# Decay attention and two expert layers on one core: another instruction order, decay rows written by engines

## The chip, the cores and the metric

One Trainium2 chip, one of its cores. A core has TensorE (PE: matmuls and transposes, with a weight load PEld ahead of each), VectorE (DVE), ScalarE (ACT), GpSimd (POOL) and SyncE (SP), on whose queue this kernel puts its DMAs. The metric is the device time of one execution in microseconds (us), as the median of several.

## The reference

```python
scores = scale * np.matmul(q, k.transpose(0, 1, 3, 2))      # 4 x 8 heads, 576 x 64
cum = np.cumsum(np.log(np.clip(f, 0.0001, 1.0)), axis=-1)
decay = cum[:, :, :, None] - cum[:, :, None, :]
scores = np.where(causal, -1000000000.0, scores + decay)
scores = scores - np.max(scores, axis=-1, keepdims=True)
attn = np.exp(scores)
attn = attn / (np.sum(attn, axis=-1, keepdims=True) + 1e-09)
x = np.matmul(attn, v)                                      # as 2304 tokens x 512
h = x @ w_in1                                               # 512 x 2048, expert layer 1
g = np.where(h >= 1, h, np.where(h <= -1, 0.0, (h + 1) ** 2 / 4))
x = g @ w_out1                                              # 2048 x 512
h = x @ w_in2                                               # expert layer 2
P = a[0] + a[1] * h + a[2] * h * h + a[3] * h * h * h
Q = 1.0 + np.abs(b[0]) * np.abs(h) + np.abs(b[1]) * h * h
out = (P / (Q + 1e-06)) @ w_out2
```

## The kernel before

Every operand of a large matmul is split into a high part, rounded to the type fp32r, and the low rest; a product is then three matmuls: low by high, high by low, high by high.

**Attention** goes through 16 pairs of heads (two heads side by side on the 128 partitions). For each pair ScalarE rounds k and q (`hi`: kh, qh), VectorE or GpSimd takes the rests (`lo`: kl, ql), and qdh/qdl hold the last 64 queries of both heads. The 576 queries are nine blocks of scores, the last one first. For a block TensorE issues the score matmuls (tiles S); VectorE adds mask and decay from `cb` and takes the row's extreme in one instruction (`max_fn`, tiles P and nm); ScalarE takes the exponential and the row sum (tile ls); TensorE transposes the block in parts of 128 (`t_fn`, tiles T, two PSUM buffers), and ScalarE or VectorE copies each transposed part to SBUF (`c_fn`, tiles PT). Then follow the products with v (tasks V, tiles O). The row sums are inverted in `r1` (a 128x9 addition of 1e-9, then the reciprocal), turned by TensorE (R2), sent through HBM and spread over the partitions (R), and GpSimd multiplies the pair's output xa by them (`r6`).

The decay of pairs 1 to 15 comes to `cb` from HBM (`cd`, which ScalarE's `c_all` fills and one DMA stores; `load_c` reads it). Pair 0 does without that trip: its decay enters the scores as a fourth matmul, of a matrix of ones with the decay rows `ct`. The cumulative sums `cum` lie in the tile `ft` (32 rows, one for each head); `c_hi` writes -8 cum rounded to fp32r, `c_lo` the rest, and two DMAs (`load_c(0)`) bring them to `ct`, whose other rows are zero. `one` is all ones, `oned` holds ones in rows 0, 1 (columns 0 to 63) and 64, 65 (columns 64 to 127). GpSimd makes these tiles with memsets.

While waiting for the first data TensorE runs `warm` matmuls on a tile of zeros, WARM + WARM2 = 26 of them.

**The expert layers** follow: layer 1 in passes over chunks of tokens (tiles h, g, a), layer 2 with its first product by a scheme of seven products of quarters, its second as three matmuls (tiles b), all behind attention except that the first matmuls of layer 1 are mixed into attention's later pairs. On the way the weights are unpacked (`w_steps`), split and stored. `root_steps` are ten small instructions (128x1) on |b[1]|, which layer 2 needs late: a square root by logarithm and exponential and two corrections.

**The order.** Every piece of work is a `task(key, engine, duration, function, deps, take, free)`. `plan` draws up a timetable from the durations given: again and again it takes, of all ready tasks, the one with the least start time plus `wk` times its key, and then the program is emitted in the order of the planned starts. So a duration in the list decides only the order; each engine runs its instructions in that order, as soon as what they depend on is done. The engine name "dve" is VectorE; "dvp" is VectorE too, but such a task and GpSimd's tasks exclude each other in the plan:

```python
at = max(clock[OF.get(eng, eng)], free_at, port[0] if eng in SHARED else 0.0)   # SHARED = ("dvp", "pool")
...
turn = SWC if ways[0][0] == "pe" and shape.get(n) != at_shape[0] else 0.0
cand = (choice[1] + turn + wk * key, key, n, choice[1], choice[2])
...
if eng == "pe" and shape.get(n) != at_shape[0]:
    at_shape[0] = shape.get(n)
    dur += SWT
```

SWC and SWT are the planned price of a turn between matmuls that take all of TensorE's rows and columns and those that take half of the rows or half of the columns. The table `NUDGE` adds an amount to the keys of runs of tasks, by their numbers.

Of the kernel before, what the change touches and what calls it, by code (L numbers as in the profile page):

```python
# [18 lines left out]
def kernel(ctx, tc, qT, kT, v, f, w_in1, w_out1, w_in2, w_out2, a, b, out):  # L19
# [9 lines left out]
    P = 128  # L29
# [21 lines left out]
    WARM, WARM2 = 12, 14  # L51
    WK = 0.025
    SWC, SWT = 0.1, 0.19
# [156 lines left out]
    POOL.memset(oned[:].bitcast(F32), 0.0)  # L210
    for j in range(2):
        pp = slice(j * QB, (j + 1) * QB)
        POOL.memset(half[pp, j:j + 1], 1.0)
        POOL.memset(oned[j * QB:j * QB + 2, pp].bitcast(F32), 1.0)
    POOL.memset(one[:].bitcast(F32), 1.0)
    POOL.memset(ct[0][:].bitcast(F32), 0.0)
# [20 lines left out]
    def load_c(pr):  # L237
        if not pr:
            for x in range(2):
                SP.dma_start(ct[0][x:P:QB, :].bitcast(F32), ft[0:2, 2 + x, :].bitcast(F32))  # L240
            return
# [26 lines left out]
    def task(key, eng, dur, fn, deps=(), take=(), free=()):  # L268
# [31 lines left out]
    ]  # L300

    def nudge(first):
        for n0, count, by_ in NUDGE:
            for n in range(max(n0, first), min(n0 + count, len(tasks))):
                if first or tasks[n][0] > -50:
                    tasks[n] = (tasks[n][0] + by_, *tasks[n][1:])
# [100 lines left out]
    def tasks_of_pair(pr):  # L407
# [37 lines left out]
        if pr:  # L445
            T("ldc", kl + 1, "sp", DC, lambda: load_c(pr), ((0, "stored"),), ("cb",))
        else:
            T("ldc", -99, "sp", [(0.55, 0.05)] * 2, lambda: load_c(pr), ((0, "c"),), ("cb",))
# [9 lines left out]
        for pos, (b, j) in enumerate(BLOCKS):  # L458
# [8 lines left out]
            def s_fn(s=s, b=b, both=both, cuts=cuts):  # L467
                if both:
                    St[s] = []
                    for n0, n1 in cuts:  # L470
                        t = psS.tile([P, 512], F32, tag="S", name=f"S{s}_{n0}")
                        ways = [(qdl[:], kh[:, n0:n1]), (qdh[:], kl_[:, n0:n1]), (qdh[:], kh[:, n0:n1])]
                        if pr == 0:
                            ways.append((oned[0:QB + 2], c_[0:QB + 2, n0:n1]))
# [98 lines left out]
        for g in (1, 0):  # L573
# [5 lines left out]
            for c in range(ncs):  # L579
# [15 lines left out]
                T(f"V{g}{c}", s0 + last + KV, "pe", mm(n - c_q, 4) + 0.03, pv_fn,  # L595
# [44 lines left out]
        T("R1", kr, "dvp", 0.25, r1, [f"E{p}" for p in range(NB)])  # L640
        T("R2", kr + 1, "pe", 0.2, r2, ("R1",), ("T",))
# [14 lines left out]
    NH = B * H  # L656
    ft = ap1.tile([NH, 4, S], F32R, tag="PT1", name="ft")
    zt = ap1.tile([NH, S], F32, tag="PT0", name="zt")
    SP.dma_start(ft[:, 0, :].bitcast(F32), f.rearrange("b h s -> (b h) s"))
# [20 lines left out]
    cum = ft[:, 1, :].bitcast(F32)  # L680

    def c_hi():
        ACT.activation(ft[:, 2, :], cum, AF.Copy, scale=-ROOT)

    def c_all():
        ACT.activation(ft[:, 0, :].bitcast(F32), cum, AF.Copy, scale=-ROOT)

    def c_lo():
        DVE.scalar_tensor_tensor(
            out=ft[:, 3, :], in0=cum, scalar=-ROOT, in1=ft[:, 2, :].bitcast(F32), op0=ALU.mult, op1=ALU.subtract  # L690
# [30 lines left out]
    x = ft[:, 0, :].bitcast(F32)  # L721
# [4 lines left out]
    t = task(-99, "act", 0.57, c_hi, (t,))  # L726
    t2 = task(-98, "act", 0.57, c_all, (t,))
# [788 lines left out]
```

## Time and profile before

| | |
|---|---|
| time, 3 runs | median 957.78 us (956.24 to 957.89) |
| the profiled execution | 958.39 us, of which the profile's span is 956.7 us |
| TensorE's mean granted clock | 0.995 |
| busy share: TensorE, VectorE, ScalarE, GpSimd | 98%, 79%, 74%, 48% |
| bytes moved by DMA | 188.55 MB, 197 GB/s |

The profile records one execution. Busy shares are of the span. The granted clock is told in parts of full speed: 1.0 is 2.4 GHz, 0.5 is 1.2 GHz. L551 in a row is line 551 of the kernel that ran. A row such as `T<-P` names the tile written and the tiles read; `[1.23 <-DVE nm]` is idle time ahead of the instruction and what ended it.

### The profile page before, as it was taken

To read this page: it belongs to the slowest core of one execution; us is meant where nothing else is said; L and a number is where in the kernel's file an instruction comes from. 1 tells how busy PE (TensorE), PEld (TensorE's weight loads), DVE (VectorE), ACT (ScalarE), POOL (GpSimd) and SP (SyncE) were. 2 spreads that over 40 slices of the span, in tenths; PEclk is the share of its full clock that TensorE was granted. 3 is DMA by queue.
4 is the path that set the end of the run, shared out by engine and by line. 5 is a ranking of instruction groups with operands and counts; after the bars stand their busy time and mean duration, and the time that the engine had idled before them with its cause. 6 is when DMAs were issued, how large, how long until landed. Compare 5 with 4: busy or idle time off the path is not lost.

```text
span 956.7 us, 16614 instructions
## 1 busy us (share of the span) xinstructions
PE 938.7 (98%) x5172; PEld 791.6 (83%) x5172; DVE 758.6 (79%) x1614; ACT 706.1 (74%) x1568; POOL 462.3 (48%) x542
## 2 busy tenths in 40 slices
PE   9899999999999999999999999999999999999998
PEld 6576877778888888878998878989899988989986
DVE  8989889983766987897658598899988888888840
ACT  7789888985665655655556589889897889878752
POOL 3666733645565422222222166666555567455553
PEclk9989999999999999999999999999999999999999
DMA  8778799755554478577947846767434464334100
GB/s 261 229 231 270 245 293 291 247 179 209 177 175 144 140 262 284 187 250 260 329 142 251 283 161 200 253 231 258 143 133 143 142 216 144 118 137 165 34 34 34
DMA packets 107345, 188.55 MB, mean 197 GB/s; under 512 B 13092, under 2 KB 43188, under 8 KB 107256
## 3 DMA queue, kind: packets, MB, share of 16 engines
q1 hardware_dynamic: 107256, 187.48, 59.0%
q8 instruction: 41, 0.67, 0.3%
q14 instruction: 48, 0.39, 0.1%
HBM read 142.72 MB, written 44.71 MB: 196 GB/s over the span
## 4 chain that ended last, share of the span: by engine, by line
PE 81%; DVE 9%; DMA 5%; ACT 2%; issue 2%; SPq 0%; DVEq 0%; ACTq 0%
PE b L1055 20%; PE h L1029 17%; PE h L777 17%; PE a L879 15%; PE T L551 3%; PE O L588 3%; PE S L485 2%; PE a L868 2%; DMA cb<-cd 1%; DVE P L527 1%; DMA wqd<-t 1%; DVE wd L109 1%; DVE arena L1000 1%; PE S L476 1%; DMA qs<-in_q_dram 1%
## 5 line engine op out<-in xcount | busy, mean ns | idle before, releaser
L798 POOL TENSOR_TENSOR gl<-t,gh 128x512 fp32r<-128x512 f32 (+2 forms) x125 | 146.7, 1179 | 213.5 <-ACT gh L793 176.3
L1055 PE MATMUL b<-w,gh 128*128 128x512 f32 x576 | 179.1, 392 | 0.0
L879 PE MATMUL a<-gh,w 128*128 128x512 f32 (+1 forms) x576 | 161.8, 366 | 0.0
L832 POOL TENSOR_TENSOR t<-t,t 128x384 f32<-128x384 f32 x96 | 99.3, 1037 | 94.9 <-ACT t L825 93.4
L1055 PEld LDWEIGHTS b<-w,gh 128*128 128x128 f32 x576 | 108.0, 188 | 21.1
L777 PE MATMUL h<-xh,arena 128*128 128x512 f32 (+1 forms) x400 | 120.0, 368 | 0.5 <-DVE t L814 0.5
L879 PEld LDWEIGHTS a<-gh,w 128*128 128x128 f32 x576 | 104.0, 189 | 17.1
L1055 PE MATMUL b<-w,gl 128*128 128x512 f32 x288 | 112.1, 389 | 0.5 <-DVE osb L399 0.5
L793 ACT CAST gh<-t 128x512 fp32r<-128x512 f32 (+2 forms) x125 | 68.8, 553 | 50.9 <-PE a L879 17.9
L879 PE MATMUL a<-gl,w 128*128 128x512 f32 (+1 forms) x288 | 105.4, 366 | 0.6 <-DVE t L890 0.5
L1029 PE MATMUL h<-arena,q 128*128 128x384 f32 x459 | 93.5, 337 | 2.9 <-DVE h L1043 1.5
L539 ACT ACTIVATE P<-P,nm 128x576 f32<-128x576 f32 (+2 forms) x144 | 83.8, 583 | 16.0 <-DVE nm L527 15.5
L814 DVE SCALAR_TENSOR_TENSOR t<-h,t 128x512 f32<-128x512 f32 (+1 forms) x77 | 47.2, 630 | 55.1 <-ACT t L809 54.9
L1029 PEld LDWEIGHTS h<-arena,q 128*128 128x128 f32 x459 | 81.1, 188 | 8.4 <-issue 1.9
L777 PEld LDWEIGHTS h<-xh,arena 128*128 128x128 f32 x400 | 73.1, 189 | 13.4 <-DVE t L814 0.9
L804 ACT ACTIVATE t<-h 128x512 f32<-128x512 f32 (+1 forms) x77 | 42.4, 551 | 50.1 <-PE h L777 49.0
L250 POOL TENSOR_SCALAR_AFFINE_SELECT cb<-cb 128x128 f32<-128x128 f32 (+1 forms) x150 | 51.0, 353 | 58.2 <-DVE nm L527 56.0
L777 PE MATMUL h<-xl,arena 128*128 128x512 f32 (+1 forms) x200 | 73.6, 368 | 0.0
L551 PE MATMUL T<-ident,P 128*128 128x128 f32 x400 | 64.7, 285 | 6.0 <-DVE PT L399 3.8
L527 DVE CUSTOM_DVE_ANT_0 P<-S,cb 128x256 f32<-128x256 f32 (+1 forms) x135 | 62.3, 476 | 7.4 <-issue 2.0
L822 ACT ACTIVATE t<-h,ab 128x384 f32<-128x384 f32 x96 | 56.1, 584 | 13.6 <-DVE h L1043 12.8
L551 PEld LDWEIGHTS T<-ident,P 128*128 128x128 f32 x400 | 46.1, 143 | 20.4 <-DVE PT L399 5.0
(185 smaller groups left out, 2332.7 us busy)
## 6 DMA issues: line engine op xcount, KB each, us to landing
q<-wqd SPq DMA_DIRECT2D x46, 512.0 KB, 3.7
raw<-in_moe_w_in_dram SPq DMA_DIRECT2D x32, 512.0 KB, 5.6
raw<-in_moe_w_out_dram SPq DMA_DIRECT2D x32, 512.0 KB, 3.8
arena<-wqd SPq DMA_DIRECT2D x26, 512.0 KB, 3.7
cb<-cd SPq DMA_DIRECT2D x15, 576.0 KB
xr<-xd SPq DMA_DIRECT2D x32, 256.0 KB, 3.6
wqd<-t SPq DMA_DIRECT2D x32, 256.0 KB, 3.8
wfd<-wd SPq DMA_DIRECT2D x26, 256.0 KB
```

Of the source, the lines that this page charges most:

```text
L250: POOL.affine_select(out=t, in_=t, compare_op=ALU.is_ge, fill=-BIG, base=0, pattern=[[-1, n]], channel_multiplier=1,)
L527: DVE.tensor_tensor_reduce(out=p[:, n0:n1], in0=t[:, 0:n1 - n0], in1=m, scale=-1.0 / ROOT, scalar=least, op0=ALU.add, op1=ALU.min, accum_o ...
L539: ACT.activation(p, p, AF.Exp, scale=-1.0, bias=nm[pr][:, pos:pos + 1], accum_out=ls[pr][:, COL[pos]:COL[pos] + 1])
L551: PE.transpose(ps[:, (c - c0) * P:(c - c0 + 1) * P], p[:, k0:k0 + P], ident[:])
L777: PE.matmul(hps[g], ww[:, kk * P:(kk + 1) * P], xx[kk], start=(kk == 0 and y == 0), stop=(kk == KD - 1 and y == 2))
L793: ACT.copy(gt[g][0], mid[g][0][:, 0:n])
L798: eng.tensor_tensor(out=lo, in0=t[:, 0:lo.shape[1]], in1=hi.bitcast(F32), op=ALU.subtract)
L822: ACT.activation(mid[g]["w"], hps[g], AF.Abs, scale=ab[:, 0:1])
L832: POOL.tensor_tensor(out=vv, in0=vv, in1=mid[g]["w"], op=ALU.add)
L879: PE.matmul(acc[x, d], ww[:, dd], gg, start=(first and y == 0), stop=(last and y == 2))
L1029: PE.matmul(o, ww, xx, start=(new and i == 0 and z == 0), stop=(i == HQ - 1 and z == 2), skip_group_check=True,)
L1055: PE.matmul(acc[x, d], gg[:, dd], ww, start=(g == 0 and y == 0), stop=(g == NF - 1 and y == 2))
```

## The change

1. Warm-up: WARM2 from 14 to 9, so 21 warm-up matmuls in place of 26.
2. First decay rows: `c_hi` and `c_lo` now write into `ct` (rows 0 to 31 high, 32 to 63 low, 64 to 95 high again, 96 to 127 a copy of the low rows by ScalarE). The two DMAs are gone. `one` is now 1 in four rows only, 0 and 32 (the first head's high and low row) and 65 and 97 (the second head's): four GpSimd instructions of 32x128 write a column of `ident` over 128 columns. `oned` takes two 64x64 copies of `one`. The fourth score matmul of the first block now uses 128 rows in place of 66. The clearing of `ct` is gone.
3. `c_all` and the store of `cd` go from keys -98 and -97 to -60.
4. In the list of durations: a V task is 4 (n - c_q) / 2400 + 0.015 in place of 4 (n / 2400 + 0.013) + 0.03, R1 is 0.33 (0.25), R2 0.12 (0.2), SWT 0.1 (0.19).
5. The root steps of VectorE are planned as "dvp".
6. The very last output tile's copy out of PSUM is done in two halves, ScalarE and VectorE.
7. `NUDGE` has 86 entries (51 before), and each has a step, so that it may shift every 77th task.

```diff
     CS = 12.0
-    WARM, WARM2 = 12, 14
+    WARM, WARM2 = 12, 9
     WK = 0.025
-    SWC, SWT = 0.1, 0.19
+    SWC, SWT = 0.1, 0.1
...
     POOL.memset(oned[:].bitcast(F32), 0.0)
+    NH = B * H
     for j in range(2):
...
         POOL.memset(half[pp, j:j + 1], 1.0)
-        POOL.memset(oned[j * QB:j * QB + 2, pp].bitcast(F32), 1.0)
-    POOL.memset(one[:].bitcast(F32), 1.0)
-    POOL.memset(ct[0][:].bitcast(F32), 0.0)
+        for x in range(2):
+            r0 = j * QB + x * NH
+            rows = slice(r0, r0 + NH)
+            POOL.tensor_scalar(
+                out=one[rows, :], in0=ident[rows, r0 + j:r0 + j + 1].to_broadcast([NH, P]), scalar1=1.0, scalar2=None,
+                op0=ALU.mult,
+            )
+        POOL.tensor_scalar(out=oned[pp, pp], in0=one[pp, pp].bitcast(F32), scalar1=1.0, scalar2=None, op0=ALU.mult)
...
     def load_c(pr):
-        if not pr:
-            for x in range(2):
-                SP.dma_start(ct[0][x:P:QB, :].bitcast(F32), ft[0:2, 2 + x, :].bitcast(F32))
-            return
         t = cb[pr % 2]
...
         for j in range(2):
...
     NUDGE = [
-        (1307, 58, 1.3), (1243, 58, 6.2), (792, 35, -3.0), (618, 16, -8.4), (1400, 59, 0.8), (884, 3, 5.1),
...
+        (23, 27, 7.2, 1), (1322, 49, 21.1, 1), (1204, 3, 2.4, 77), (57, 8, -20.5, 77), (1430, 18, 5.5, 1),
...
     ]
...
     def nudge(first):
-        for n0, count, by_ in NUDGE:
-            for n in range(max(n0, first), min(n0 + count, len(tasks))):
-                if first or tasks[n][0] > -50:
+        for n0, count, by_, step_ in NUDGE:
+            for n in range(n0, min(n0 + count * step_, len(tasks)), step_):
+                if n >= first and n0 >= first and (first or tasks[n][0] > -50):
                     tasks[n] = (tasks[n][0] + by_, *tasks[n][1:])
...
         else:
-            T("ldc", -99, "sp", [(0.55, 0.05)] * 2, lambda: load_c(pr), ((0, "c"),), ("cb",))
+            T("ldc", -99, "act", 0.57, lambda: ACT.copy(ct[0][P - NH:P, :], ct[0][NH:2 * NH, :].bitcast(F32)), ("c", "c2"), ("cb",))
         ways, lo_, qd_ = (["dvp", "pool"], [0.68, 1.42], [0.24, 0.4]) if pr else (["dvp"], [0.68], [0.24])
...
             kk += 15 * x * (not pr)
...
                         if pr == 0:
-                            ways.append((oned[0:QB + 2], c_[0:QB + 2, n0:n1]))
+                            ways.append((oned[:], c_[:, n0:n1]))
                         for x, (lhs, rhs) in enumerate(ways):
...
                         St[s].append((t, n0, n1))
...
-                T(f"V{g}{c}", s0 + last + KV, "pe", mm(n - c_q, 4) + 0.03, pv_fn,
+                T(f"V{g}{c}", s0 + last + KV, "pe", 4 * (n - c_q) / 2400 + 0.015, pv_fn,
                   deps + ["ldv"] + ([f"V{g}{c - 1}"] if c else []) + (["V14"] if g == 0 else []), ("O",) if c == 0 else (),
...
                 shape[tid[pr, f"V{g}{c}"]] = "columns"
...
         kr = s0 + NB - 1 + KR
-        T("R1", kr, "dvp", 0.25, r1, [f"E{p}" for p in range(NB)])
-        T("R2", kr + 1, "pe", 0.2, r2, ("R1",), ("T",))
+        T("R1", kr, "dvp", 0.33, r1, [f"E{p}" for p in range(NB)])
+        T("R2", kr + 1, "pe", 0.12, r2, ("R1",), ("T",))
         T("R3", kr + 1, "act", 0.16, r3, ("R2",), (), ("T",))
...
         T("R5", kr + 6, "sp", [(0.55, 0.4), (0.55, 0.05)] * 2, r5, ("R4",), ("R",))
...
-    NH = B * H
-    ft = ap1.tile([NH, 4, S], F32R, tag="PT1", name="ft")
+    ft = ap1.tile([NH, 2, S], F32, tag="PT1", name="ft")
     zt = ap1.tile([NH, S], F32, tag="PT0", name="zt")
-    SP.dma_start(ft[:, 0, :].bitcast(F32), f.rearrange("b h s -> (b h) s"))
+    SP.dma_start(ft[:, 0, :], f.rearrange("b h s -> (b h) s"))
     still = ap1.tile([P, 512], mybir.dt.bfloat16, tag="P", name="still", bufs=PB)
...
     DVE.memset(zt[:], 0.0)
...
-    cum = ft[:, 1, :].bitcast(F32)
-    def c_hi():
-        ACT.activation(ft[:, 2, :], cum, AF.Copy, scale=-ROOT)
+    cum = ft[:, 1, :]
+    def c_hi(r0):
+        ACT.activation(ct[0][r0:r0 + NH, :], cum, AF.Copy, scale=-ROOT)
     def c_all():
-        ACT.activation(ft[:, 0, :].bitcast(F32), cum, AF.Copy, scale=-ROOT)
+        ACT.activation(ft[:, 0, :], cum, AF.Copy, scale=-ROOT)
...
         DVE.scalar_tensor_tensor(
-            out=ft[:, 3, :], in0=cum, scalar=-ROOT, in1=ft[:, 2, :].bitcast(F32), op0=ALU.mult, op1=ALU.subtract
+            out=ct[0][NH:2 * NH, :], in0=cum, scalar=-ROOT, in1=ct[0][0:NH, :].bitcast(F32), op0=ALU.mult, op1=ALU.subtract
         )
...
     task(-99, "pe", 0.22 * WARM2, lambda: warm(WARM2), (t,), ("T",), ("T",))
-    x = ft[:, 0, :].bitcast(F32)
+    x = ft[:, 0, :]
     t = task(-99, "init", 2.86, lambda: None)
...
     t = task(-99, "dve", 1.35, lambda x=x: f_scan(cum, x), (t,))
-    t = task(-99, "act", 0.57, c_hi, (t,))
-    t2 = task(-98, "act", 0.57, c_all, (t,))
-    t = tid[0, "c"] = task(-99, "dve", 0.67, c_lo, (t,))
+    t2 = task(-99, "act", 0.57, lambda: c_hi(0), (t,))
+    tid[0, "c2"] = task(-99, "act", 0.57, lambda: c_hi(QB), (t,))
+    t3 = task(-60, "act", 0.57, c_all, (t,))
+    t = tid[0, "c"] = task(-99, "dve", 0.67, c_lo, (t2,))
     tid[0, "stored"] = task(
-        -97, "sp", [(0.55, 0.1)], lambda: SP.dma_start(cd.rearrange("r (j s) -> (r j) s", j=2), ft[:, 0, :].bitcast(F32)), (t2, t)
+        -60, "sp", [(0.55, 0.1)], lambda: SP.dma_start(cd.rearrange("r (j s) -> (r j) s", j=2), ft[:, 0, :]), (t3,)
     )
...
     for e, fn in root_steps():
-        t = task(30, e, 0.3 if e == "act" else 0.17, fn, (t,))
+        t = task(30, "act" if e == "act" else "dvp", 0.3 if e == "act" else 0.17, fn, (t,))
...
...
         os_[x, d] = t_new("o", "t2", DM, TN[2]) if d == 2 else stage.tile([P, DM], F32, tag="d", name="osb", bufs=2)[:]
-        copy(eng, os_[x, d], acc.pop((x, d)))
+        a = acc.pop((x, d))
+        if eng == "both":
+            copy("act", os_[x, d][:, 0:DM // 2], a[:, 0:DM // 2])
+            copy("dve", os_[x, d][:, DM // 2:], a[:, DM // 2:])
+        else:
+            copy(eng, os_[x, d], a)
...
                     eng = ("act", "dve")[d % 2]
-                    o = task(key, eng, cost(eng, DM, "ps"), lambda x=x, d=d, eng=eng: out_copy(x, d, eng), (tout,), (("d", "d", "t2")[d],), (f"a{d}",))
+                    to = "both" if n == 2 * NSUP - 1 and d == QN // P - 1 else eng
+                    o = task(key, eng, cost(eng, DM, "ps"), lambda x=x, d=d, to=to: out_copy(x, d, to), (tout,), (("d", "d", "t2")[d],), (f"a{d}",))
                     task(key, "sp", ld(DM), lambda x=x, d=d: out_store(x, d), (o,), (), (("d", "d", "t2")[d],))
```

The change moves instructions on every engine. Three places follow; a row is line, operation, tile written, tiles read and the shape, and "x2" stands for two in a row. A number behind a name only tells apart tiles of one name.

**GpSimd, the start of the program**, up to the first mask of pair 1 (one_139 is `one`, one_140 is `oned`, kl_117 and kl_119 the rests of k for even and odd pairs). Before:

```order
L210 MEMSET one_140 128x128
L213 MEMSET half 64x1 x2
L215 MEMSET one_139 128x128
L214 MEMSET one_140 2x64 x2
L216 MEMSET ct_130 128x576
L435 TENSOR_TENSOR kl_117<-ks_218,kh_116 128x576
L250 AFFINE_SELECT cb_129<-cb_129 64x64 x2
```

After:

```order
L210 MEMSET one_140 128x128
L215 MEMSET half 64x1
L219 TENSOR_SCALAR one_139<-ident 32x128 x2
L215 MEMSET half 64x1
L219 TENSOR_SCALAR one_139<-ident 32x128
L223 TENSOR_SCALAR one_140<-one_139 64x64
L219 TENSOR_SCALAR one_139<-ident 32x128
L446 TENSOR_TENSOR kl_119<-ks_187,kh_118 128x576
L223 TENSOR_SCALAR one_140<-one_139 64x64
L253 AFFINE_SELECT cb_129<-cb_129 64x64 x2
```

The clearing of `ct` is gone, `one` and `oned` are made by TENSOR_SCALAR, and kl_119, of pair 1, now stands ahead of the second half of `oned`; before, `oned` was complete ahead of any kl.

**ScalarE, the start of the program**, from the logarithm of f to the rounding of pair 1's q and k (ft is the tile of the cumulative sums, ct_130 the decay rows of pair 0; kh_116, qh_120 belong to pair 0, kh_118, qh_122 to pair 1). Before:

```order
L724 ACTIVATE ft<-ft 32x576
L431 CAST kh_116<-ks_158 128x576
L431 CAST qh_120<-qs_160 128x576
L683 ACTIVATE ft<-ft 32x576
L686 ACTIVATE ft<-ft 32x576
L431 CAST kh_118<-ks_181 128x576
L431 CAST qh_122<-qs_185 128x576
```

After:

```order
L734 ACTIVATE ft<-ft 32x576
L442 CAST kh_116<-ks_160 128x576
L442 CAST qh_120<-qs_162 128x576
L693 ACTIVATE ct_130<-ft 32x576 x2
L459 CAST ct_130<-ct_130 32x576
L696 ACTIVATE ft<-ft 32x576
L442 CAST qh_122<-qs_180 128x576
L442 CAST kh_118<-ks_187 128x576
```

There are now two writes of high decay rows and a copy of the low ones (the CAST row) ahead of the whole rows (ACTIVATE ft), and pair 1's q stands ahead of its k.

**VectorE, the place of the second set of root steps** (rt, 128x1), among copies of transposes (PT), the score reductions (ISA, two rows each) and, after the change, a step of unpacking a weight (wd). Before:

```order
L712 RECIPROCAL rt<-rt 128x1
L399 COPY PT_1_698<-T_4_703 128x2x64
L713 SCALAR_TENSOR_TENSOR rt<-rt,ab 128x1
L399 COPY PT_1_698<-T_0_705 128x4x128
L527 ISA P_729,nm_573<-S_0_655,cb_128 128x256
L527 ISA nm_573 128x1
L527 ISA P_742,nm_573<-S_0_656,cb_128 128x256
```

After:

```order
L410 COPY PT_1_864<-T_0_931 128x3x128
L722 RECIPROCAL rt<-rt 128x1
L115 SCALAR_TENSOR_TENSOR wd<-raw_1_0_414,wd 128x512
L723 SCALAR_TENSOR_TENSOR rt<-rt,ab 128x1
L724 TENSOR_SCALAR rt<-rt 128x1
L538 ISA P_983,nm_791<-S_0_867,cb_129 128x128
L538 ISA nm_791 128x1
L722 RECIPROCAL rt<-rt 128x1
L538 ISA P_991,nm_791<-S_0_868,cb_129 128x128
```

The reciprocal, the product and the scaling now stand between other neighbours: a weight step ahead of the product, a reduction ahead of the next reciprocal.

## Rows read from the trace of the kernel before

**Rows 1.** The page: busy time, and the granted clock in 40 slices.

```profile
PE 938.7 (98%) x5172; PEld 791.6 (83%) x5172; DVE 758.6 (79%) x1614; ACT 706.1 (74%) x1568; POOL 462.3 (48%) x542
...
PEclk9989999999999999999999999999999999999999
```

**Rows 2.** Waits of TensorE over the whole span: us in total, times, longest us.

```profile
PE T L551 <- DVE PT L399: 3.8, 7, 0.8
...
PE S L485 <- DVE nm L527: 1.2, 1, 1.2
...
PE T L551 <- ACT PT L397: 1.0, 4, 0.3
```

**Rows 3.** Stretches, TensorE alone: length, busy (count), granted clock, DMA share, GB/s.

```profile
25.00:95.00 70.00, 63.47 (x502) 0.95 0.78 244
95.00:215.00 120.00, 118.17 (x887) 1.00 0.79 250
```

**Rows 4.** Timeline of TensorE, the first matmul of the expert layers: start, length in us.

```profile
95.33 0.48 PE L777 MATMUL h<-xh,w 128*128 128x512 f32 x1
```

**Rows 5.** Timeline of the first 16 us, five engines: start, length, idle time before.

```profile
1.26 8.07 PE L670 MATMUL warm<-still 128*128 128x512 bf16 x26 [1.26 <-DVE still L661]
...
2.25 0.54 POOL L185 TENSOR_SCALAR_AFFINE_SELECT tri<-tri 64x64 f32<-64x64 f32 x2
...
5.51 0.68 ACT L683 ACTIVATE ft<-ft 32x576 fp32r<-32x576 f32 x1
...
6.22 0.75 DVE L689 SCALAR_TENSOR_TENSOR ft<-ft 32x576 fp32r<-32x576 f32 x1 [0.35 <-ACT ft L683]
...
7.76 0.27 DVE L438 TENSOR_TENSOR qdl<-ql,half 128x128 fp32r<-128x128 f32 x1
...
8.98 0.50 PE L476 MATMUL S<-kh,qdl 128*128 128x320 f32 x1
...
9.60 0.31 PE L476 MATMUL S<-ct,one 66*128 66x320 f32 x1
...
15.22 1.42 POOL L435 TENSOR_TENSOR kl<-ks,kh 128x576 fp32r<-128x576 f32 x1 [9.97 <-ACT kh L431]
```

**Rows 6.** Timeline from 35 to 47 us, VectorE, GpSimd and TensorE.

```profile
35.36 1.47 DVE L713 SCALAR_TENSOR_TENSOR rt<-rt,ab 128x1 f32<-128x1 f32 x1
...
35.40 1.42 POOL L637 TENSOR_TENSOR xa<-xa,R 128x576 f32<-128x576 f32 x1
...
42.59 1.30 POOL L137 TENSOR_TENSOR w<-wd,w 128x512 fp32r<-128x512 f32 x1 [2.14 <-ACT w L133]
...
42.93 0.98 DVE L612 TENSOR_SCALAR rt<-ls 128x9 f32<-128x9 f32 x1
...
43.84 1.41 POOL L637 TENSOR_TENSOR xa<-xa,R 128x576 f32<-128x576 f32 x1
...
44.08 1.19 DVE L713 SCALAR_TENSOR_TENSOR rt<-rt,ab 128x1 f32<-128x1 f32 x1
...
46.84 1.19 PE L485 MATMUL S<-kh,ql 64*128 64x256 f32 x3 [1.23 <-DVE nm L527]
```

**Rows 7.** Line L612: duration in ns min/median/max, first and last start in us.

```profile
L612 DVE TENSOR_SCALAR rt<-ls x16: 159/213/1095, 18.5 to 209.5; 128x9 f32<-128x9 f32 x16
```

**Rows 8.** Timeline, the copy of the last output tile.

```profile
952.83 0.58 ACT L397 COPY t_o<-b 128x512 f32<-128x512 f32 x1 [0.77 <-PE b L1055]
```

**Rows 9.** Stretches around the fall of the clock, TensorE alone, columns as in 3.

```profile
35.00:40.00 5.00, 3.60 (x27) 1.00 0.67 232
...
45.00:46.80 1.80, 0.61 (x4) 1.00 1.03 301
46.80:50.20 3.40, 3.32 (x18) 0.51 0.95 364
50.20:53.70 3.50, 3.50 (x18) 0.50 0.03 13
53.70:60.00 6.30, 6.30 (x60) 1.00 0.61 185
```

25 rows, old and new, of the table NUDGE are left out of this document.

## The prediction, made before the changed kernel was run

> **What bounds the kernel now.** I read the profile from the whole to the place. First the busy shares: TensorE is busy 98% of the span, and the granted clock is at its upper level (2.4 GHz) in nearly every slice [rows 1]. So every gain has to come from the little time in which TensorE stands still or runs slowly. The list of TensorE's waits says for whom it stands: transposes wait for VectorE or ScalarE to copy the previous transposes out of PSUM, and score matmuls wait for VectorE's reduction [rows 2]. Then a table of stretches says where: from 25 to 95 us TensorE is idle 70 - 63.47 = 6.5 us (0.093 per us), from 95 to 215 us only 1.8 us (0.015 per us) [rows 3]. The difference is that the first expert layer's matmuls start at 95.33 us and fill the gaps of attention from there on [rows 4]. The timeline of the first 10 us shows the start [rows 5], and the timeline around 40 us what VectorE did before TensorE's worst wait [rows 6].
>
> TensorE issues the same matmuls in both programs, less five warm-up ones. So the sum has only changes of waits in it.
>
> **The change part by part.**
>
> *The start: +1.6 us.* Now 26 warm-up matmuls keep TensorE until the first score matmul at 8.98 us; its operands were ready earlier, since the last of them (qd's low part) ends at 7.76 + 0.27 = 8.03 us. The next three follow at once, and the fourth, which takes the decay rows (ct) and the matrix of ones, starts at 9.60 us [rows 5]. With five warm-ups fewer, at 8.07 / 26 = 0.31 us mean (the late, fast ones less), the first score matmul could start at about 8.1 us. But the fourth matmul needs the second half of `oned`, and the order listing of GpSimd shows that half behind kl of pair 1. That instruction waits for kh of pair 1, which ScalarE now does after the copy of the low decay rows, the whole decay rows and qh of pair 1. Step by step: ScalarE's first decay instruction starts at 5.51 as now, VectorE's low part starts at 6.22 and takes 0.75, so to 6.97; then the copy (0.6), the whole rows (0.6), qh (0.6) and kh (0.68 to its end), each at ScalarE's 0.68 us for 32x576 less some overlap: 9.45 us. GpSimd's kl takes 1.42 us: 10.9 us. The 64x64 write of `oned` has no row in this trace; a GpSimd row of 64x64 (two affine selects in 0.54 us) gives 0.27 each, and I take 0.25, between nothing and 0.4 (about the whole pair). The fourth matmul then starts at 11.2 us in place of 9.60: +1.6, bounds +1.3 to +1.9. Behind it on TensorE stands every other score matmul, and behind those VectorE's reductions and ScalarE's exponentials, so I let all of it reach the end. GpSimd's four writes of `one` before that cost nothing: before its first kl it now stands idle for 9.97 us [rows 5], and they lie in that time; without that cover they would cost about 0.3 us each, by the affine select. The two transfers of decay rows that fall away free SP's queue; in their place the k load that reuses pair 1's buffer now stands ahead of pair 1's decay broadcast and waits for GpSimd's kl, so that broadcast is issued at 11.3 us or later. I cost it at nothing, because pair 1's masks come behind all of pair 0's output in the new order; without that cover each us of lateness is one us.
>
> *Small VectorE steps off GpSimd's time: -3.1 us.* The product of the square root steps is 128x1 and took 1.47 and 1.19 us; both times it ended together with a GpSimd two-operand instruction that ran meanwhile (35.40 + 1.42 = 36.82, 43.84 + 1.41 = 45.25). The row sums' first step (128x9) took 0.98 us at 42.93, until GpSimd's 42.59 + 1.30 = 43.89 [rows 6]; elsewhere it takes 0.16 to 0.27 [rows 7]. Against 0.16 each that is 1.31 + 1.03 + 0.82 = 3.16 us of VectorE. VectorE has no idle time between them, and the score matmul at 46.84 us is released by the reduction behind them after 1.23 us of waiting [rows 6], so I let all of it count. The list now plans these steps as instructions that must not meet GpSimd. Bounds: -4.1 (with the one of 1.10 us, the largest of [rows 7]) and 0, if they meet GpSimd again at other places.
>
> *The order of everything else.* Three terms. (a) Transposes in a row: a third or later block must wait until the first one's copy has left the two PSUM buffers. The order listing of TensorE has 11 such blocks now and 18 after. TensorE waited 3.8 + 1.0 = 4.8 us in 11 waits for such copies [rows 2], 0.44 us each; seven more would be +3.1. Second blocks fall from 78 to 68. I take +1.2, between 0 and +3.1, a little under the middle, because the ten second blocks fewer take some of it back. (b) The first expert matmul stands 75 matmuls earlier in TensorE's order, which is 9.5 us at 63.47 / 502 = 0.126 us for one in that stretch [rows 3]; those 9.5 us go from 0.093 idle per us to 0.015: -0.7, bounds -1.5 and 0. (c) Corrected durations in the list (V's matmuls, R2, the turn between shapes) move no work; what they do to the remaining waits I can't work out row by row, and carry as 0 with bounds of 3 us to either side, half of the 6.5 us that TensorE is idle from 25 to 95 us.
>
> *The end: -0.2 us.* The last output tile's copy takes 0.58 us on ScalarE [rows 8] and is split in two halves of 256 on two engines. ScalarE's own half would take 0.36 (an estimate: half of 0.58 and a fixed part), VectorE's a little more: -0.17, bounds -0.3 and 0.
>
> The sum: +1.6 - 3.1 + 1.2 - 0.7 - 0.2 = -1.2 us. The profiled execution took 958.39 us (956.7 of span and 1.7 around it), which gives 957.2. It lies 0.6 above the median of the runs, 957.78; on that, **956.6 us**.
>
> **The clock, and the rivals.** From 46.8 to 53.7 us the granted clock is 0.5, that is the lower level of 1.2 GHz; before it fell TensorE had been busy 0.61 us of 1.80 [rows 9]. In those 6.9 us 36 matmuls start, and in the next 6.3 us 60 [rows 9]: 36 at that pace are 3.8 us, so the fall costs 3.1 us, at most half of 6.9 = 3.45. The new start has the same shape: TensorE does three score matmuls, to about 8.6 us, and then stands until 11.2, for 2.6 us. The forecast holds one fall of the clock, as now, at the one place or the other.
>
> The Trainium skill's page "TensorE: Matmul & The Clock Gate" (section "HAM oscillation — how this bites in real kernels") says that a TensorE which waits too long between bursts of matmuls drops to half its clock and must earn it back. By that rule the stall at the start costs a fall of its own, on top of the 1.6 us; the sum would be 956.6 + 3.4 = 960.0. The fall at 46.8 us agrees with the rule; the stretch from 35 to 40 us, with TensorE busy 3.60 of 5.00 us in parts and the clock at its upper level throughout [rows 9], shows that not every wait brings a fall, and by it the sum stays at 956.6.
>
> *Rival A, no fall at all:* the steps that held up VectorE before 46.8 us are gone, TensorE no longer stands there, and the start's stall does not drop the clock. For it: the 3.1 us of VectorE lie just ahead of that wait. Against: the start. Time: 956.6 - 3.4 = 953.2 us.
>
> *Rival B, slower:* the stall at the start drops the clock and the fall near 47 us stays, since the new order also has long runs of transposes there. Price: 3.4 us more, TensorE having nothing beside it at the start that could hide it; 960.0 us. It decides when TensorE is granted 0.5 for one stretch more than now; the point from which it makes the kernel slower is a loss of 3.1 us beyond the forecast.
>
> *Rival C, the change doesn't do what it says:* the list keeps the small steps off GpSimd's planned time, but the engines don't run by the plan, and the steps meet GpSimd elsewhere. For it: nothing in the trace ties GpSimd's starts to VectorE's, so a plan that is off by one us brings them together again. Against it: the listing of VectorE has the steps at other places, between reductions. Then the -3.1 falls away: 959.7 us, no change that could be told.
>
> **How the numbers follow.** A measurement of this kernel can tell 0.2%, 1.9 us: faster is under 955.9, slower over 959.7. Forecast 0.40 (its own range, by the bounds of its terms taken half, 954.5 to 958.7), rival A 0.25, B 0.17, C 0.18. Faster: A whole, and 0.17 of the forecast's 0.40: 0.42. Slower: most of B and something under half of C: 0.22. Same: 0.36. The range leaves out a tenth on either side: from 952.2, a us beyond A, to 960.7, a little beyond B.
>
> **What would show it.** The fourth score matmul starts at about 11.2 us, released by GpSimd, with 2.6 us of TensorE's idle time before it; if it starts before 9.6, the first term is wrong. The root steps and the row sums' steps take 0.15 to 0.27 us each; any over 0.9 us speaks for C. The first expert matmul starts about 85 us. TensorE's waits for copies of transposes sum to about 6 us. The granted clock has one stretch of 0.5 before the end; none is A, two is B. The prediction is wrong if attention's end (the last O matmul, near 214 us now) moves by more than 4 us, or if anything after 215 us moves by more than 1.

## The result, and the profile after

The changed kernel takes **964.04 us** (median of five, 962.47 to 965.41), the kernel before 957.78: a ratio of 1.0070 with the interval 1.0055 to 1.0085. It is slower, outside the predicted range, and on the other side of the forecast. (The table of the change has 82 entries, not 86 as the section on the change says.) The profiled execution took 964.04 us too, with a span of 962.3 in place of 956.7: 5.6 us to be found.

The page of the changed kernel, busy time and granted clock, as [rows 1]:

```profile
PE 938.7 (98%) x5167; PEld 790.4 (82%) x5167; DVE 758.1 (79%) x1603; ACT 710.4 (74%) x1580; POOL 469.4 (49%) x546
...
PEclk8999999999999999999999999999999999999999
```

TensorE's busy time is the same in sum, so its idle time has grown by 5.6 us. The sum hides a shift, though: five warm-ups fewer take 2.0 us of busy time away (8.07 us before, 6.03 now), and the other matmuls keep TensorE busy as much longer. The fall of the clock has moved from the third slice to the first. To split the span, take the last O matmul, since in both programs exactly 3625 matmuls stand from it on. Tile O before and in the changed kernel (duration min/median/max in ns, first and last start in us), then the last matmul before and the end of the changed kernel's timeline:

```profile
L588 PE MATMUL O<-PT,vt x448: 219/382/689, 18.2 to 214.4; 128*64 128x320 f32 x64, 128*64 128x192 f32 x22, 128*64 128x128 f32 x22, 128*64 128x64 f32 x21
L599 PE MATMUL O<-PT,vt x448: 219/380/484, 25.2 to 216.4; 128*64 128x320 f32 x64, 128*64 128x64 f32 x23, 128*64 128x192 f32 x22, 128*64 128x128 f32 x21
```

```profile
952.17 0.61 PE L1055 MATMUL b<-w,gh 128*128 128x512 f32 x2
```

```profile
957.88 0.61 PE L1071 MATMUL b<-w,gh 128*128 128x512 f32 x2
958.53 0.37 ACT L408 COPY t_o<-b 128x256 f32<-128x256 f32 x1 [0.77 <-PE b L1071]
958.94 0.42 DVE L410 COPY t_o<-b 128x256 f32<-128x256 f32 x1 [0.39 <-ACT t_o L408]
959.39 0.33 SPq L919 DMA_DIRECT2D out_dram<-t_o  x1
```

In the kernel before the last O matmul starts at 214.4 us and the last matmul ends at 952.8 (952.17 + 0.61). So attention got 2.0 us longer (216.4 against 214.4), everything from there to the last matmul 3.7 us longer (958.5 - 216.4 = 742.1 against 738.4), and the rest of the span is 3.8 us against 3.9. TensorE alone in the stretch behind attention, before and after (length, busy and count, granted clock, DMA share, GB/s):

```profile
214.38:952.79 738.41, 733.95 (x3630) 1.00 0.54 182
```

```profile
216.35:958.49 742.14, 735.15 (x3630) 1.00 0.55 183
```

Of the 3.7 us, 2.5 are idle time (4.5 us before, 7.0 now), and for 1.2 us more TensorE is busy with the same matmuls at the same clock. What makes them longer in the new order these profiles don't show.

The start of the changed kernel, as [rows 5]:

```profile
1.26 6.03 PE L680 MATMUL warm<-still 128*128 128x512 bf16 x21 [1.26 <-DVE still L671]
...
3.99 3.47 POOL L219 TENSOR_SCALAR one<-ident 32x128 fp32r<-32x128 f32 x2
...
8.51 0.38 PE L487 MATMUL S<-kh,qdl 128*128 128x320 f32 x1 [1.22 <-ACT ft L696]
...
8.96 0.67 ACT L442 CAST kh<-ks 128x576 fp32r<-128x576 f32 x1
...
9.76 1.53 POOL L446 TENSOR_TENSOR kl<-ks,kh 128x576 fp32r<-128x576 f32 x1 [0.46 <-POOL one L219]
...
11.38 0.37 POOL L223 TENSOR_SCALAR one<-one 64x64 fp32r<-64x64 f32 x1
11.80 0.63 PE L487 MATMUL S<-ct,one 128*128 128x320 f32 x1 [2.62 <-POOL one L223]
```

The fourth score matmul starts at 11.80 us, released by GpSimd's second half of `oned`, which stood behind kl. TensorE had been without work for 2.62 us. Stretches of the changed kernel, TensorE alone, columns as in [rows 3]:

```profile
8.50:11.80 3.30, 0.68 (x3) 0.85 1.02 380
11.80:18.40 6.60, 6.60 (x39) 0.56 0.69 244
18.40:25.00 6.60, 5.33 (x42) 1.00 0.80 206
25.00:95.00 70.00, 63.73 (x502) 1.00 0.76 234
95.00:215.00 120.00, 119.83 (x929) 1.00 0.75 244
215.00:540.00 325.00, 319.80 (x1593) 1.00 0.65 218
540.00:700.00 160.00, 158.21 (x783) 1.00 0.67 218
700.00:953.00 253.00, 253.00 (x1249) 1.00 0.36 119
```

The clock is at its lower level in most of 11.8 to 18.4 us and at 1.00 from 25 us on, where [rows 9] had the fall. Behind attention the kernel before had these rows:

```profile
215.00:540.00 325.00, 323.93 (x1607) 1.00 0.64 218
540.00:700.00 160.00, 156.62 (x776) 1.00 0.63 212
700.00:953.00 253.00, 252.79 (x1245) 1.00 0.35 116
```

From 215 to 540 us TensorE now stands idle for 5.2 us in place of 1.1, and gets 1.6 back by 700. TensorE's waits over the whole span, as [rows 2]:

```profile
PE T L562 <- ACT PT L408: 3.0, 8, 0.6
PE S L487 <- POOL one L223: 2.6, 1, 2.6
PE T L562 <- DVE PT L410: 2.6, 4, 1.5
PE a L890 <- DVE t L901: 2.3, 2, 2.1
PE a L890 <- POOL gl L809: 1.3, 1, 1.3
PE b L1071 <- DVE osb L410: 1.3, 1, 1.3
...
PE h L788 <- DVE xl L776: 1.1, 2, 0.9
```

Four of these lie behind attention, from a to h; all the waits there sum to 7.0 us. Before, they summed to 4.4, the longest 1.5 for another tile.

### The profile page after: what moved, and what is told of

Same layout as the page of the kernel before. It is cut to its first block, busy times and chain, and to the rows that moved or that the text cites. A ratio compares the mean times of both kernels' runs of the same rounds, so it can differ in the third digit from the quotient of the medians.

```text
span 962.3 us, 16619 instructions
## 1 busy us (share of the span) xinstructions
PE 938.7 (98%) x5167; PEld 790.4 (82%) x5167; DVE 758.1 (79%) x1603; ACT 710.4 (74%) x1580; POOL 469.4 (49%) x546
## 4 chain that ended last, share of the span: by engine, by line
PE 84%; DVE 6%; DMA 3%; ACT 3%; issue 2%; POOL 0%; SPq 0%; DVEq 0%; ACTq 0%; POOLq 0%
PE b L1071 20%; PE h L1045 18%; PE h L788 17%; PE a L890 14%; PE O L599 5%; PE T L562 4%; PE S L496 3%; PE a L879 2%; PE S L487 1%; DVE wd L109 1%; DVE wd L103 1%; ACT P L550 1%; DMA cb<-cd 1%; DVE wd L99 1%; DVE arena L1016 1%
## 5 line engine op out<-in xcount | busy, mean ns | idle before, releaser
L809 POOL TENSOR_TENSOR gl<-t,gh 128x512 fp32r<-128x512 f32 (+2 forms) x120 | 142.4, 1191 | 208.1 <-ACT gh L804 135.6
L1045 PE MATMUL h<-arena,q 128*128 128x384 f32 x513 | 104.1, 336 | 0.5 <-ACT gh L804 0.3
L804 ACT CAST gh<-t 128x512 fp32r<-128x512 f32 (+2 forms) x120 | 66.3, 555 | 42.7 <-PE a L890 16.7
L1045 PEld LDWEIGHTS h<-arena,q 128*128 128x128 f32 x513 | 91.1, 188 | 5.2 <-ACT arena L1012 0.7
L890 PEld LDWEIGHTS a<-gl,w 128*128 128x128 f32 x288 | 54.3, 189 | 12.7 <-issue 2.5
```

What stands on the lines that cost most here:

```text
L804: ACT.copy(gt[g][0], mid[g][0][:, 0:n])
L809: eng.tensor_tensor(out=lo, in0=t[:, 0:lo.shape[1]], in1=hi.bitcast(F32), op=ALU.subtract)
L890: PE.matmul(acc[x, d], ww[:, dd], gg, start=(first and y == 0), stop=(last and y == 2))
L1045: PE.matmul(o, ww, xx, start=(new and i == 0 and z == 0), stop=(i == HQ - 1 and z == 2), skip_group_check=True,)
```

## The experiments

Theory 1: the stall at the start, with its fall of the clock, and the new order behind attention each cost several us. Theory 2 (the rival): only the order does, and the late start is swallowed by later waits. Each time is a median with its ratio to the kernel before on the same chip.

**The start.** First, `one` and `oned` are written ahead of every planned task, so that on GpSimd alone kl moves behind `oned`:

```diff
-        for x in range(2):
...
-        POOL.tensor_scalar(out=oned[pp, pp], in0=one[pp, pp].bitcast(F32), scalar1=1.0, scalar2=None, op0=ALU.mult)
...
     man.enter_context(tc.manual_schedule())
+    for j in range(2):
+        pp = slice(j * QB, (j + 1) * QB)
+        for x in range(2):
...
+        POOL.tensor_scalar(out=oned[pp, pp], in0=one[pp, pp].bitcast(F32), scalar1=1.0, scalar2=None, op0=ALU.mult)
```

> The changed kernel with one thing moved: GpSimd writes both halves of oned ahead of pair 1's kl. Every other engine's order is the same. Theory 1 (the start's stall and its fall of the clock carry through to the end): in the changed kernel the fourth score matmul starts at 11.80 us and TensorE stands still for 2.6 us before it; now it should start at about 9.5, when GpSimd's last write is done, with no stretch of granted clock 0.5 at 12 to 18 us. That is 2.3 us less of lateness and 3.4 us of clock: 964.0 - 5.7 = 958.3. If the clock then falls at another place instead, 961.7. Theory 2 (the loss lies in the new order, and later waits swallow the late start): 964.

960.38 us (957.21 to 962.04), ratio 1.0032 [1.0019, 1.0045]. Its start:

```profile
8.71 0.31 PE L479 MATMUL S<-kh,qdh 128*128 128x320 f32 x1
10.01 0.42 PE L479 MATMUL S<-ct,one 128*128 128x320 f32 x1 [0.99 <-POOL one L667]
```

No fall of the clock at the start, but one between 74 and 80 us (0.72 there; it is at the lower level from 76.2 to 79.6): nearest to the case of 961.7. TensorE's order is the same as in the changed kernel, so each matmul can be compared with the same one. How much later the changed kernel starts it than this experiment (matmuls counted without the warm-ups):

```
matmul           4th    13th   31st   261st  461st  501st  1522nd
later by, us     1.79   2.84   4.06   3.99   4.50   3.30   3.31
```

1.8 us of lateness become 4.06 while the clock is low, and from there on the distance stays as it is through 190 us of attention; it changes at 64 us, by one wait, and around 78 us, where the experiment has its own fall of the clock. Nothing swallows the late start: theory 2 falls for this part.

Second, the decay rows of before in the new order (`one`, `oned` and `ct` by memsets, two DMAs, 66 rows, 26 warm-ups):

```diff
-            T("ldc", -99, "act", 0.57, lambda: ACT.copy(ct[0][P - NH:P, :], ct[0][NH:2 * NH, :].bitcast(F32)), ("c", "c2"), ("cb",))
+            T("ldc", -99, "act", 0.57, lambda: [SP.dma_start(ct[0][x:P:QB, :].bitcast(F32), ft[0:2, 2 + x, :].bitcast(F32)) for x in range(2)], ("c", "c2"), ("cb",))
```

> The changed kernel in its own order, with the decay rows of before (two DMAs, memsets, 66 rows) and 26 warm-up matmuls. Theory 1: the fourth score matmul starts near 9.6 to 9.9 (the two DMAs stand later on the queue), no stall of 2.6 us, no fall of the clock at 12 us: 964.0 - 2.0 - 3.4 = 958.6. Theory 2, the loss lies in the new order: 964.

960.73 us, 1.0039 [1.0024, 1.0054], 2.1 above the expected 958.6. The fourth score matmul came later than expected, at 11.13 us, released by the DMA. But TensorE stood only 0.79 us before it and the profile, which is of the fastest of seven executions, shows no low clock in attention: the last O matmul starts at 212.6. The distance to the first experiment is 1.12 us at the fourth matmul and 1.09 until the 461st. Lateness alone costs itself; the rest of the changed kernel's 4.06 us is the clock.

Third, the reverse: the new decay rows and 21 warm-ups in the exact order of before.

```diff
-            for x in range(2):
-                SP.dma_start(ct[0][x:P:QB, :].bitcast(F32), ft[0:2, 2 + x, :].bitcast(F32))
+            ACT.copy(ct[0][P - NH:P, :], ct[0][NH:2 * NH, :].bitcast(F32))
             return
```

> The kernel before, in its own order, with the decay rows written by engines, one and oned made from the identity (both ahead of any kl) and 21 warm-up matmuls. Theory 1: the fourth score matmul starts at about 9.5 in place of 9.60, so nothing moves: 957.7; the stretch of clock 0.5 at 47 us stays. Theory 2, in which the start has no part in the loss, says the same, 957.8. A time over 960 would say that the new decay rows cost something beyond the place of kl (GpSimd's writes, ScalarE's copies).

956.84 us, 0.9997 [0.9987, 1.0007]; fourth score matmul at 9.19. The new rows cost nothing where `oned` is in time, and five warm-ups fewer bring nothing.

**The order behind attention.** First, the entries of before for the second plan:

> The changed kernel with the table entries of before for the second plan (all that follows attention, from about 217 us). Up to there every engine's order is that of the changed kernel. In the profile of the changed kernel TensorE stands still for 7.0 us from 215 to 953 us, in that of before for 4.7. Theory 1, those 2.3 us come from the new entries: 964.0 - 2.3 = 961.7, with the wait of 2.1 us near 416 us gone. Rival: they come from how attention hands over to the expert layers, or from chance in one execution: 964.

```diff
-        (2779, 6, 7.3, 1), (3414, 18, -0.1, 1), (3321, 16, -6.3, 1), (2702, 169, 1.5, 1), (3471, 10, 5.5, 1),
...
+        (2778, 10, 9.9, 1), (4791, 81, 0.8, 1), (3415, 52, -1.1, 1), (3320, 16, -6.2, 1), (4958, 174, 0.1, 1),
```

977.36 us, 1.0208 [1.0190, 1.0226]: neither theory. Old entries on another timetable give a third order, worse than both. Such a run says nothing of where 3.7 us lie; the order itself has to be put in. So the next two carry the order as a list, attention of the one kernel and the rest of the other (in the second of them with + for -):

```diff
-    order_ = plan(first, WKB)
+    order_ = [(x // 4 - 1, tasks[x // 4 - 1][1][x % 4][2]) for x in REPLAY]
```

> The kernel before up to the end of attention, then every engine's instructions in the changed kernel's order (the order is given as a list). From the start of the last O matmul to the end of the last matmul the kernel before takes 738.4 us, the changed one 742.1. Theory 1, that order alone costs the 3.7 us: the stretch takes 742 and the whole 957.2 + 3.7 = 960.9. Rival, the waits come from how the changed attention leaves buffers and transfers: 738.4 and 957.2.

959.98 us, 1.0037 [1.0024, 1.0051]; last O matmul at 213.7, the stretch behind it 741.6. Its waits of TensorE behind attention:

```profile
PE a L879 <- POOL gl L798: 2.2, 1, 2.2
PE a L879 <- DVE t L890: 1.7, 1, 1.7
PE b L1055 <- DVE osb L399: 1.3, 1, 1.3
```

These are the waits of the changed kernel, behind the old attention: the order brings them, and the stretch is 3.2 us longer than before.

> The changed kernel with oned ahead of pair 1's kl (the first experiment, 960.4), and after attention every engine's instructions in the order of the kernel before. Theory 1: the stretch after the last O matmul takes 738.4 again, the whole 960.4 - 3.7 = 956.7. Rival: the stretch stays at 742 and the whole at 960.4.

957.02 us, 0.9999 [0.9991, 1.0008]; last O matmul at 212.4, the stretch 740.0, with one wait of the changed kernel left (the second row, VectorE's xl near 221 us):

```profile
PE h L1048 <- DVE h L1062: 1.5, 1, 1.5
PE h L791 <- DVE xl L779: 1.1, 1, 1.1
PE h L791 <- DVE t L828: 0.8, 1, 0.8
```

So 2.1 us leave with the order. The other 1.6 stay though the order is that of before; 1.1 of them is the wait for xl, right behind attention. That they come from how attention hands over is argued from that place and not shown. The two experiments together put the share of the order at 2.1 to 3.2 us of the 3.7, so both theories hold a part. The medians agree that the order is the larger one: from the first experiment to this one, which differ in nothing else, the time falls by 3.4 us. Last, the corrected durations (SWT, V, R1, R2) alone in the kernel before:

```diff
-                T(f"V{g}{c}", s0 + last + KV, "pe", mm(n - c_q, 4) + 0.03, pv_fn,
+                T(f"V{g}{c}", s0 + last + KV, "pe", 4 * (n - c_q) / 2400 + 0.015, pv_fn,
```

> The kernel before with the four durations of the change (V, SWT, R1, R2) and its own table. If corrected durations give a better order by themselves: under 956. If the table only fits the timetable that it was made for, as the old entries behind the new attention say (977), the entries now shift keys at the wrong places: over 962. If neither matters much: 957.

982.36 us, 1.0257 [1.0234, 1.0281]: last O matmul at 222.5, the stretch behind it 752.8 (3621 matmuls there). A table of shifts belongs to one timetable.

**The small steps of VectorE.** The kernel before with its root steps held back until attention is over:

```diff
         for n, fn in order:
-            fn()
+            if n not in roots:
+                fn()
```

> The kernel before with the ten root steps issued right after attention in place of 35 to 46 us; nothing else is moved. The prediction's term: two of these steps were held up by GpSimd for 1.31 and 1.03 us, and VectorE had no idle time behind them, so the last O matmul should start 2.3 us earlier (212.0 in place of 214.4) and the whole take 957.2 - 2.3 = 954.9, less still if the clock no longer falls at 47 us (953). Rival: TensorE waits there for something else, 957.2.

956.21 us, 0.9994 [0.9985, 1.0003]; last O matmul at 213.7, as in the other profile with the old attention as it was (213.7, above). VectorE at the place of [rows 6], before, and then VectorE and GpSimd in this kernel:

```profile
45.43 0.75 DVE L435 TENSOR_TENSOR ql<-qs,qh 128x576 fp32r<-128x576 f32 x1
46.10 0.68 DVE L527 CUSTOM_DVE_ANT_0 P<-S,cb 128x512 f32<-128x512 f32 x1
```

```profile
43.01 1.25 DVE L612 TENSOR_SCALAR rt<-ls 128x9 f32<-128x9 f32 x1
44.29 0.22 DVE L613 RECIPROCAL rt<-rt 128x9 f32<-128x9 f32 x1
44.42 1.78 DVE L435 TENSOR_TENSOR ql<-qs,qh 128x576 fp32r<-128x576 f32 x1
46.13 0.68 DVE L527 CUSTOM_DVE_ANT_0 P<-S,cb 128x512 f32<-128x512 f32 x1
```

```profile
42.93 1.30 POOL L137 TENSOR_TENSOR w<-wd,w 128x512 fp32r<-128x512 f32 x1 [2.14 <-ACT w L133]
44.18 1.41 POOL L637 TENSOR_TENSOR xa<-xa,R 128x576 f32<-128x576 f32 x1
```

The root step that took 1.19 us is gone, and ql behind it takes 1.78 us, where 0.75 is usual for it. The reduction starts at 46.13; in the kernel before it was 46.10. Here the 1 us that VectorE loses goes with GpSimd's instruction and falls on the next step. At the other place, where the product took 1.47 us, no step of VectorE takes the loss over, but VectorE now waits 0.43 us for a transpose and then 0.45 us for GpSimd's mask:

```profile
37.51 0.42 DVE L527 CUSTOM_DVE_ANT_0 P<-S,cb 128x256 f32<-128x256 f32 x1 [0.45 <-POOL cb L250]
```

Counted from the reduction that starts at 33.78 us (33.29 before), this one comes 0.34 us earlier than before, of the 1.31 that went with the product.

**Attempts at a better kernel**, all with the new attention and the old order behind it (957.02). `one` written by ScalarE, `oned` by VectorE:

```diff
+            ACT.copy(one[rows, :], ident[rows, r0 + j:r0 + j + 1].to_broadcast([NH, P]))
...
+            DVE.tensor_copy(oned[pp, pp], one[pp, pp].bitcast(F32))
```

> As the one with the old order after attention, but one is written by ScalarE while it waits for the first data and oned by VectorE, none of it by GpSimd, whose writes of 32x128 took up to 3.2 us for two while VectorE worked. The fourth score matmul should start at about 9.0 us in place of 10.01. If a later start of attention goes through to the end: 956.7 - 1.0 = 955.7, and 954 where no fall of the clock comes. If later waits swallow it: 956.7.

957.87 us, 1.0008 [0.9998, 1.0017]: the fourth score matmul starts at 9.12 (9.34 in the profile that it is compared with), and nothing is won. Then VectorE's pair 1 work behind pair 0's third reduction, its splits of x ahead of a weight's unpacking, and both:

```diff
+    behind([tid[1, x] for x in ("qlo", "qd0", "qd1")], tid[0, "M2"])
+    behind(sx0[2:], sx0[1])
```

> The kernel with the new attention and the old order behind it (957.0), where VectorE does pair 1's ql, qdh and qdl after the third score reduction of pair 0 in place of before the first. In that kernel qdl took 1.51 us because GpSimd's kl of pair 1 ran at the same time, and the first reduction started at 11.71 us though its scores were there by 10. Theory: the first reduction starts near 10.2, and that 1.5 us goes through to the end of attention as the start's lateness did: last O 212.4 - 1.5 = 210.9, whole 955.5. Rival: the next step that meets kl is held up in its place, or TensorE waits later for pair 1's scores: 957.

957.72 us, 1.0010 [1.0001, 1.0019]. The first reduction starts at 10.63 in place of 11.71, and the 19th matmul 1.07 us earlier; by the 55th matmul 0.29 of it is left.

> The same kernel, where VectorE splits the last two parts of x right behind the second one, ahead of four steps of unpacking a weight (2.2 us). TensorE waits 1.08 us for that split near 221 us. Theory: this wait goes and the stretch from the last O matmul to the last matmul falls from 740.0 to 738.9: 957.0 - 1.1 = 955.9. Rival: the late weight gives a wait further on, 957.

957.33 us, 1.0007 [0.9998, 1.0016]. The wait near 221 us is gone; the next split of x gives another:

```profile
234.47 0.50 PE L791 MATMUL h<-xl,w 128*128 128x512 f32 x1 [0.81 <-DVE xl L779]
```

> Both moves together: 957.0 - 1.5 - 1.1 = 954.4, 0.997 of the kernel before, if both go through; 955.7 if one does.

957.51 us, 1.0009 [1.0001, 1.0018]. Each move does what it should at its place and is given back behind it. All four medians come out slightly above that of the kernel that they start from. The profiles show one thing: the one that they are compared with has no fall of the clock before the last matmul, and each of the four has one of 3.4 us between 63 and 80 us. Whether more than that is behind it stays open. No version beats the kernel before by more than its interval.

## Why the prediction was wrong

Of the 7.4 us between the forecast and the result 3.7 lie behind attention, 3.0 in attention (-1.0 forecast, 2.0 measured), 0.1 at the end, and 0.6 is what the forecast took off for the median.

**The order of everything else (c)** is the step that failed: "what they do to the remaining waits I can't work out row by row, and carry as 0", with bounds taken from the idle time of 25 to 95 us, and "nothing after 215 us" moving by more than 1. Of the table's 82 entries 52 work behind attention. There the stretch is 3.7 us longer; the order brought 3.2 when it was put behind the old attention, and taking it out behind the new one gave back 2.1. The prediction works out no row of the order there, where TensorE was idle for 4.5 us in 738. Little idle time says what there is to win, not what a new order can lose. "So the sum has only changes of waits in it" failed there too: 1.2 of the 3.7 us are the same matmuls taking longer.

**The start** was right in its mechanism and mis-sized: 11.80 us in place of 11.2 for the fourth score matmul, and 2.62 us of idle time as forecast. Every link was a little longer than worked out: kh ended at 9.63 us (9.45), kl took 1.53 us (1.42), `oned` 0.37 (0.25). GpSimd's writes of `one`, costed at nothing, weren't free either: with kl out of the way, in the first experiment's profile, it is they that hold the fourth matmul until 10.01 us. (In the sixth experiment, with the same start, they happened to be shorter and the fourth matmul starts at 9.34 with no wait.) The fall of the clock at the start, weighed as a possibility, came, and the one near 47 us did not; one stretch, as the forecast held. At the start the low clock cost 4.06 - 1.79 = 2.3 us that stayed through attention, less than the 3.1 to 3.45 of the prediction and about what a fall as long costs the kernel before (last section). What differs is how often it comes: all five executions of the changed kernel had a mean granted clock of 0.995 or 0.996, while part of those of the kernel before had no fall. The Trainium skill's page "TensorE: Matmul & The Clock Gate" (section "HAM oscillation — how this bites in real kernels") says that a TensorE which waits too long between bursts of matmuls drops to half its clock; the row 11.80 to 18.40 agrees.

**The small steps of VectorE, -3.1 us**, failed in the reasoning: the steps are short now (the two products 0.24 and 0.88 us, the row sums' step at most 0.46), but the holdup wasn't theirs. Taken out alone, two of them brought no change that could be told, where 2.3 us were expected. The Trainium skill's page "SBUF — State Buffer" (section "SBUF: two separate sides") says that GpSimd and VectorE, in some of its instructions such as those with two inputs from SBUF, lock one pair of ports for a whole instruction and the loser waits; 1.25 and 1.78 us agree with that. That a moved step hands its wait to the next one is what the rows at 44 us show; at 36 us another wait ended the gain.

**Transposes in a row, +1.2**: the waits for copies are 5.6 us in 12 (4.8 in 11 before), +0.8. **First expert matmul**: 86.6 us in the sixth experiment, where the start is in time (90.5 in the changed kernel); forecast 85. TensorE's idle time from 95 to 215 us fell from 1.8 to 0.2. With the start mended the last O matmul of the new attention starts at 212.4 to 213.7 us in seven profiles (mean 213.2), of the old at 213.7 to 214.4 in four (mean 214.0): 0.8 us. But two of the seven have no fall of the clock in attention, and one of the four has a longer one; among profiles with one fall of 3.4 us it is 213.4 (five) against 213.9 (three). So 0.4 to 0.8 us is won, at most a third of the 2.6 counted for the small steps, transposes and expert matmuls together. **The end, -0.2**: the two halves run one behind the other, VectorE released by ScalarE, and the store is issued 0.86 us after the first copy starts, 0.61 before; the time from the last matmul's end stays 3.8 to 3.9.

## What to carry to other kernels

When a table changes an order, read the listing where the engine waits least as well: a stretch without idle time can only lose. Here a late start of the engine that bounds the kernel was not made up again: the 4.06 us of the 31st matmul shrank, to 3.31, only where the other profile had a fall of the clock of its own. A head start was not kept like that: 1.07 us became 0.29 within some 35 matmuls. So the first few instructions of every engine deserve to be followed one by one, with the clock of the stretch behind a wait in the sum. Before a stretched step is counted as a gain, ask which instruction of another engine stretches it, and who stands next.

## What was unexpected of the hardware

- VectorE's qdl (128x128, 0.28 us as a rule) took 1.51 us when it met GpSimd's kl at the start of the sixth experiment; the first reduction stood behind it.
- GpSimd's copy of 32x128 took 0.53 to 2.26 us in the changed kernel, beside VectorE's scan, splits and decay rows.
- The fall of the clock comes in some executions only, and its length differs. Of 23 executions of the kernel before that ran beside the first experiments, 7 had a mean granted clock of 1.000, median 955.7 us. Nine had 0.998 (as in the profiles of the third, fifth and eighth experiments, whose low stretch is 3.4 us long), median 957.4; four had 0.996, median 958.35, which fits a low stretch of 6.8 us as in [rows 9]; three had 0.997. So a fall costs about 1.7 us when it is short and 2.7 when it is long, not 3.1 to 3.45; in all 90 executions beside the experiments the same groups differ by 1.1 and 2.1 us.
